# The opening of a transformer block: row statistics and products first on VectorE, PSUM copies by the free engine, values of three groups of heads computed there

## The chip, the cores and the metric

One core of a Trainium2 chip runs the whole kernel. Its engines work from queues of their own and wait for each other by semaphores: TensorE (PE in the profile, its weight loads PEld) multiplies matrices into PSUM, VectorE (DVE), ScalarE (ACT) and GpSimd (POOL) compute, and SyncE (SP) issues the transfers. The metric is the device time of one execution in microseconds (us): 1263.09 us before, the median of three runs (1261.11 to 1264.53).

## The reference

A pre-norm transformer block over 2048 tokens of width 1024, 32 heads of 32 columns, feed-forward width 3584, all tensors bf16:

```python
x = A_x
h = x + attention(layernorm(x), wqkv, wo)     # softmax(q k^T / sqrt(32)) v, all 32 heads
h2 = h + gelu(layernorm(h) @ w1 + b1) @ w2 + b2
```

The layer norm subtracts the row's mean and divides by the root of its variance plus 1e-5; it has no weights.

## The kernel before, in words

**Tiles and groups.** The tokens are 16 row tiles of 128 (`NT`) and four chunks `tc` of 512 (`NCH`). The 1024 columns of queries, keys and values are eight groups of 128 columns, four heads each (`G`); a group is two pairs of heads. A projection of one group for one chunk is eight matmuls of 512 columns into one PSUM bank and one copy out of it: `proj_k`, `proj_q`, `proj_v`. This text calls it a set. A key set is copied to a staging slot `kst` (five slots, `NKS`), squared on VectorE into `sqk` (L563), and carried by four DMAs to `K2`. A query set is copied to `QT` and squared into `sqq` (L579). A value set is copied to `kst` and turned by one DMA transpose into `V` (L597).

**A planner writes the order.** The Python code does not issue instructions directly. `plan.task` appends each to the list of its engine with the waits that its buffers ask for, and keeps an estimated time at which each engine comes free (`plan.free`). The order on each engine is then fixed, and the engine follows it strictly: an instruction that waits holds up all behind it. Steps that can be placed at leisure lie in chains. `service(t)` goes through the chains in list order and records the first step of each whose inputs and engine are about to be free at the estimated time t.

**The head** is all that happens until the first score matmul. Its parts, in the order of the data:

1. SyncE issues the loads of the 16 row tiles `xr` and of nine weight slots `wk` (L710 to L720).
2. `ln1_batch` (L673) handles two row tiles at a time. Statistics are two halves and an aggregate on VectorE (L455, L457); twelve small steps on GpSimd work out the inverse deviation (L475 to L491), and VectorE takes its reciprocal (L492). Then ScalarE subtracts the mean (L685, 1024 columns) and VectorE multiplies (L688). The chain of the statistics is an ordinary one; the chain of subtract and multiply is put in front of it (`first`).
3. `ln1_tp` (L697) transposes the tile by eight TensorE instructions (L498) into a bank, and ScalarE copies it to `xnT` (L702).
4. When a chunk's four tiles are there, TensorE can do the key set of group 0, in chunk 0 also the query sets of groups 0 to 3, and the value set of group 0. ScalarE copies all of these out of PSUM (L555, L576, L594). The squares L563 and L579 are recorded on VectorE at the moment the set is recorded, behind nothing but what was recorded earlier.
5. `qnorm_a`, `qnorm_b`, `knorm_a` and `knorm_b` make the bound that softmax subtracts: a small matmul over the squares (L608), a maximum on VectorE (L611), a diagonal on VectorE (L619), a matmul that spreads it (L621), and a maximum (L623).

The loop at L741 chooses what TensorE does next: among the candidates in `cands` whose inputs are ready, the lowest number goes first (0 the transposes, 1 keys and norms, 2 queries, 3 values). It ends when the norms of the first queries and of key group 0 are recorded.

**After the head** come four phases, one for each chunk of queries. In a phase, 16 pairs of heads pass, each in 11 units. A unit is three score matmul tiles (L919), one exponential on ScalarE over 1536 columns (L927), and the products with values and with ones (L956). Between them TensorE does filler work out of `fill0` (L780): the rest of the projections, in the order of the groups, one PSUM bank (number 7) being left for it, copied out by VectorE. A pair of group g can't begin before the key norm of group g is there: `qk_prereq` calls `until(("kn", g))`, which does filler work without a pause until it is. In phases 1 to 3 the filler is the output projection and feed-forward of the chunk before; the last feed-forward is the tail.

Of the kernel before, what the change touches and what calls it, by code (L numbers as in the profile page):

```python
# [8 lines left out]
ACT = mybir.ActivationFunctionType  # L9
# [4 lines left out]
P = 128  # L14
# [187 lines left out]
def build_kernel(nc, A_x, A_wqkv, A_wo, B_w1, B_b1, B_w2, B_b2, out):  # L202
# [199 lines left out]
    def record_step(ch):  # L402
        eng, fn, reads, writes, cost = ch.steps.popleft()
        if eng == "mark":
            if fn not in marks:
                until(fn)
        elif eng == "call":
            fn()
        else:
            plan.task(eng, fn, reads=reads, writes=writes, cost=cost)  # L410
# [7 lines left out]
    def service(t):  # L418
        again = True
        while again:  # L420
            again = False
            for ch in list(chains):
                eng, fn, reads, writes, cost = ch.steps[0]
                if eng == "mark":
                    ok = fn in marks
                elif eng == "call":
                    ok = plan.ready(E.SP, reads, writes) <= t
                else:
                    r = plan.ready(eng, reads, writes)
                    if eng == E.DVE:  # L430
                        ok = plan.free[eng] <= t + 250 and r <= t + 250
                    else:
                        ok = r <= max(plan.free[eng], t)
                if ok:
                    record_step(ch)
                    again = True
                    if not ch.steps:
                        chains.remove(ch)

    def chain(steps, first=False):  # L440
        ch = Chain(steps)
        if first:
            k = sum(1 for c_ in chains if c_.first)
            chains.insert(k, ch)
            ch.first = True
        else:
            chains.append(ch)
        return ch
# [60 lines left out]
    def group(mms, evac, reads_of, n=512, chunk=2, chs=()):  # L509
        bank = fbanks.next()  # L510
        k = len(mms)
        for i, (lhsT, rhs) in enumerate(mms):
# [7 lines left out]
            if i == k - 1:  # L520
                evac(bank)


    wslot = {}
    wfree = deque(range(NWK))
    worder = deque([("k", 0)] + [("q", g) for g in range(4)] + [("v", 0)]
                   + [(k_, g) for g in range(1, 4) for k_ in "kv"] + [("q", g) for g in range(4, 8)]
                   + [(k_, g) for g in range(4, 8) for k_ in "kv"] + [("Q", g) for g in range(G)])

    def load_next():  # L530
# [14 lines left out]

    kscount = [0]

    def proj_k(g, tc, eng="dve"):
        s = wslot[("k", g)]

        def evac(bank):
            ks = kscount[0] % NKS
            kscount[0] += 1
            if eng == "act":
                act(lambda a: a.activation(kst[:, ks, :], ps[:, bank, :], ACT.Copy), reads=[B_ps[bank]], writes=[B_kst[ks]], cost=600)  # L555
            else:
                dve(lambda v: v.tensor_copy(kst[:, ks, :], ps[:, bank, :]), reads=[B_ps[bank]], writes=[B_kst[ks]], cost=690)
            src = kst[:, ks, :].rearrange("p (a b c) -> p a b c", a=2, b=2)
            for pr in range(2):
                for par in range(2):  # L560
                    dma(K2[64 * par:64 * par + 64, 2 * g + pr, 2 * tc:2 * tc + 2, :], src[64 * pr:64 * pr + 64, :, par, :], 32768,
                        reads=[B_kst[ks]], writes=[B_K2h[2 * g + pr][tc][par]], lanes=lanes_q)
            dve(lambda v: v.tensor_tensor(sqk[:, tc, :], kst[:, ks, :], kst[:, ks, :], ALU.mult),  # L563
                reads=[B_kst[ks]], writes=[B_sqk[tc]], cost=420)
            marks.add(("k", g, tc))

        yield from group([(wk[:, s, dc, :], xnT[tc][:, dc, :]) for dc in range(DC)], evac,
                         lambda i: [B_wk[s]] + xn_of(tc))

    def proj_q(g, tc, eng="dve", late=None, key="q"):  # L570
        s = wslot[(key, g)]
        w_, B_w, q2, B_q2 = (wk, B_wk, sqq, B_sqq) if late is None else late

        def evac(bank):
            if eng == "act":
                act(lambda a: a.activation(QT[:, QS[tc], g, :], ps[:, bank, :], ACT.Copy), reads=[B_ps[bank]], writes=[B_QT[tc][g]], cost=600)  # L576
            else:
                dve(lambda v: v.tensor_copy(QT[:, QS[tc], g, :], ps[:, bank, :]), reads=[B_ps[bank]], writes=[B_QT[tc][g]], cost=690)
            dve(lambda v: v.tensor_tensor(q2[:, g % 4, :], QT[:, QS[tc], g, :], QT[:, QS[tc], g, :], ALU.mult),  # L579
                reads=[B_QT[tc][g]], writes=[B_q2[g % 4]], cost=420)  # L580
            marks.add(("q", g, tc))

        yield from group([(w_[:, s, dc, :], xnT[tc][:, dc, :]) for dc in range(DC)], evac,
                         lambda i: [B_w[s]] + xn_of(tc))

    def proj_v(g, tc, eng="dve"):

        s = wslot[("v", g)]

        def evac(bank):  # L590
            ks = kscount[0] % NKS
            kscount[0] += 1
            if eng == "act":
                act(lambda a: a.activation(kst[:, ks, :], ps[:, bank, :], ACT.Copy), reads=[B_ps[bank]], writes=[B_kst[ks]], cost=600)  # L594
            else:
                dve(lambda v: v.tensor_copy(kst[:, ks, :], ps[:, bank, :]), reads=[B_ps[bank]], writes=[B_kst[ks]], cost=690)
            dma_t(V[:, tc * 4:tc * 4 + 4, g * P:(g + 1) * P], kst[:, ks, :], 131072, [B_kst[ks]], [B_V[tc * 4 + t][g] for t in range(4)])  # L597
# [75 lines left out]
    def ln1_batch(tiles):  # L673
# [3 lines left out]
            st += ln_stats_steps(s_, tt % 4, xrt[tt], B_xr[tt])  # L677
        lo, hi = tiles[0] % 4, tiles[-1] % 4 + 1
        k = s_ * 2 + lo // 2
        rs = ln_rstd_steps(s_, lo, hi, E.Pool, -1.0)  # L680

        def spawn():
            for tt in tiles:
                x_ap, B_x, i = xrt[tt], B_xr[tt], tt % 4
                chain([(E.Activation, lambda a, x_ap=x_ap, i=i: a.activation(x_ap, x_ap, ACT.Identity, bias=lnf[:, s_, i, 0:1], scale=-1.0),  # L685
                        [B_x, B_lnm[k]], [B_x], 1080),
                       ("mark", ("rs", k), [], [], 0),
                       (E.DVE, lambda v, x_ap=x_ap, i=i: v.tensor_scalar(x_ap, x_ap, rstd[:, s_, i:i + 1], None, ALU.mult),  # L688
                        [B_x, B_rstd[k]], [B_x], 430),
                       ("call", lambda tt=tt: normed.add(tt), [], [], 0) if tt < TP else  # L690
                       ("call", lambda tt=tt: ln1_t(tt), [B_x], [B_xnTf[tt]], 0)], True)
        chain(st + rs[:1] + [("call", spawn, [], [], 0)] + rs[1:] + [("call", lambda: marks.add(("rs", k)), [], [], 0)])

    TP = 16
    normed = set()

    def ln1_tp(tt):  # L697
# [1 line left out]
        bank = fbanks.next()  # L699
        yield Need([B_xr[tt]], [B_ps[bank]])  # L700
        tp = transposes(lambda k: xrt[tt][:, k * P:(k + 1) * P], [B_xr[tt]], bank, DC)
        act(lambda a: a.activation(xnT[tc][:, :, t4 * P:(t4 + 1) * P], tp.rearrange("p (dc t) -> p dc t", dc=DC), ACT.Copy),  # L702
            reads=[B_ps[bank]], writes=[B_xnTf[tt]], cost=980)
        marks.add(("xn", tt))

    def ln1_t(tt):
        dma_t(xnT[tt // 4][:, :, (tt % 4) * P:(tt % 4 + 1) * P], xrt[tt], 262144, [B_xr[tt]], [B_xnTf[tt]])
        marks.add(("xn", tt))

    for tt in range(4):  # L710
# [7 lines left out]
        load_x(tt)  # L718
    for _ in range(4):
        load_next()  # L720
    for tt in range(0, NT, 2):
        ln1_batch([tt, tt + 1])

    cands = []
    for tt in range(TP):
        cands.append((0, lambda tt=tt: tt in normed, [B_xr[tt]], ln1_tp(tt)))
    for tc in range(NCH):
        def got(tc=tc):
            return all(("xn", t_) in marks for t_ in range(tc * 4, tc * 4 + 4))
        cands.append((1, got, xn_of(tc), proj_k(0, tc, "act")))  # L730
        if tc == 0:
            for g in range(4):
                cands.append((2, got, xn_of(tc), proj_q(g, 0, "act")))
    cands.append((1, lambda: all(("q", g, 0) in marks for g in range(4)), B_sqq, qnorm_a(0, 0)))
    cands.append((1, lambda: B_qn[0].w is not None, [B_qn[0]], qnorm_b(0, 0)))
    cands.append((1, lambda: all(("k", 0, tc) in marks for tc in range(NCH)), B_sqk, knorm_a(0)))
    cands.append((1, lambda: B_kn[0].w is not None, [B_kn[0]], knorm_b(0)))
    for tc in range(NCH):
        cands.append((3, lambda tc=tc: all(("xn", t_) in marks for t_ in range(tc * 4, tc * 4 + 4)), xn_of(tc), proj_v(0, tc, "act")))
    clock = 0.0  # L740
    while ("kn", 0) not in marks or ("qn", 0, 0) not in marks:  # L741
        clock = max(clock, plan.free[E.PE])
# [12 lines left out]
        if ("q", 0, 0) in marks:  # L755
            qd_load(0, 0)
            qd_load(0, 1)
    v_left = [c_[3] for c_ in cands if c_[0] == 3]
    with_b = [("b1", b1bf, B_b1, Bf_b1bf), ("b2", b2bf, B_b2, Bf_b2bf)]
    for _, t_, src, B_ in with_b:  # L760
        dma(t_[:], src.rearrange("(c p) -> p c", p=P), 8192, writes=[B_], lanes=lanes_a, noncontig=True)
# [18 lines left out]
    def fill0():  # L780
        for key in [("k", 0)] + [("q", g) for g in range(4)]:
            used(key)
        for gen in v_left:
            yield from gen
        used(("v", 0))

        def keys(g, side=()):
            side = deque(side)
# [4 lines left out]
            used(("k", g))  # L793

        def values(g):
            for tc in range(NCH):
                yield from proj_v(g, tc)
                if tc < 2:
                    yield from (knorm_a, knorm_b)[tc](g)
            used(("v", g))  # L800

        for g in range(1, 4):
            yield from keys(g)
# [708 lines left out]
```

## Time and profile before

| | us |
|---|---|
| median of three runs | 1263.09 |
| the profiled execution | 1257.86 |
| its span, first to last instruction | 1255.6 |
| first transposes on TensorE | 10.91 |
| first projection matmul | 17.23 |
| first score matmul (end of the head) | 61.28 |
| first exponential | 62.02 |
| first exponential of phase 1 | 326.45 |
| TensorE busy over the span | 1171.9 |
| ScalarE busy over the span | 1120.8 |
| VectorE busy over the span | 636.6 |

Times in the profile are from the span's start. A timeline row gives the start, the duration, the engine, the line, what is written and read, and in brackets how long the engine was idle before it and what released it. Rows of like instructions in sequence are merged (x2 and so on). A table by windows gives each engine's busy time in stretches of the span, with the number of instructions in parentheses; PEclk is the granted TensorE clock as a share of full speed, and the last columns are the busy share of the DMA engines and GB/s. Durations overlap where an engine pipelines, so the distance from start to start is the cost of an instruction in a row of them.

### The profile page before, as it was taken

The numbers are of one execution on the slowest core, as the hardware profiler recorded it, in microseconds if no ns is written. First come the engines' busy times: TensorE is split into PE (matmuls) and PEld (weight loads), VectorE is DVE, ScalarE is ACT, GpSimd is POOL, SyncE is SP. The second block draws the span as 40 slices with busy tenths as digits, with TensorE's granted clock in tenths as the row PEclk, the third lists the DMA queues.
The fourth block names the chain that finished last, engine by engine and source line by source line (L and its number), as shares of the span: only waits on it lengthen the run. The fifth ranks groups of instructions, "written<-read, shape, count | busy, mean of one in ns | idle before, by whom it ended". The sixth has DMA issues, their size and how long they took to land.

```text
span 1255.6 us, 22538 instructions
## 1 busy us (share of the span) xinstructions
PE 1171.9 (93%) x9066; PEld 399.6 (32%) x9232; DVE 636.6 (51%) x1181; ACT 1120.8 (89%) x914; POOL 36.0 (3%) x180
## 2 busy tenths in 40 slices
PE   5699998999999999999999999999999999997998
PEld 3333322333233333333333332333222323333444
DVE  6524444444465878222366884222568842236820
ACT  6799997999999999999999999999999999962831
POOL 3300000000010000000010000000100000000000
PEclk9899999999999999999999999999999999997999
DMA  7162222223341324343623251342223513334733
GB/s 222 28 129 64 60 61 62 58 59 80 101 68 55 93 72 118 76 114 77 177 47 93 77 151 39 76 121 71 63 76 90 138 35 80 97 85 134 193 89 92
DMA packets 316056, 113.70 MB, mean 91 GB/s; under 512 B 235568, under 2 KB 313392, under 8 KB 315952
## 3 DMA queue, kind: packets, MB, share of 16 engines
q1 hardware_dynamic: 315952, 112.25, 35.8%
q8 instruction: 73, 1.20, 0.4%
q14 instruction: 31, 0.25, 0.1%
HBM read 84.94 MB, written 4.19 MB: 71 GB/s over the span
## 4 chain that ended last, share of the span: by engine, by line
PE 77%; DVE 8%; ACT 8%; issue 6%; DMA 1%; POOL 0%; DVEq 0%; SPq 0%; ACTq 0%
PE ps L518 29%; PE ps L956 16%; PE ps L1251 15%; PE ps L919 15%; ACT PT L927 6%; DVE xh L1218 1%; DVE lnst L455 1%; ACT tm L1227 1%; DVE Rg L976 1%; DVE QT L986 0%; DVE tm L1225 0%; PE ps L498 0%; DVE Sg L969 0%; DVE rcp L979 0%; DVE tm L1224 0%
## 5 line engine op out<-in xcount | busy, mean ns | idle before, releaser
L927 ACT ACTIVATE PT<-ps,biasm 128x1536 bf16<-128x1536 f32 (+1 forms) x704 | 996.6, 1545 | 24.5 <-PE ps L919 21.6
L956 PE MATMUL ps<-PT,ones 128*32 128x512 bf16 x2048 | 285.7, 384 | 0.0
L956 PE MATMUL ps<-PT,V 128*32 128x512 bf16 x2048 | 285.4, 384 | 0.3
L919 PE MATMUL ps<-Qd,K 32*128 32x512 bf16 x2048 | 274.6, 386 | 8.4 <-ACT PT L927 6.3
L518 PE MATMUL ps<-hnT,w 128*128 128x512 bf16 x629 | 165.8, 382 | 9.3 <-issue 3.5
L1251 PE MATMUL ps<-gT,w 128*128 128x512 bf16 x629 | 166.2, 381 | 6.2 <-issue 5.2
L919 PEld LDWEIGHTS ps<-Qd,K 32*128 32x128 bf16 x2048 | 68.0, 91 | 292.7 <-issue 149.1
L956 PEld LDWEIGHTS ps<-PT,V 128*32 128x32 bf16 x2048 | 77.0, 95 | 142.0 <-issue 95.2
L969 DVE COPY Sg<-ps 128x512 f32<-128x512 f32 x64 | 44.3, 692 | 152.9 <-PE ps L956 152.9
L518 PE MATMUL ps<-xnTe,wk 128*128 128x512 bf16 x357 | 94.2, 387 | 6.4 <-issue 1.7
L1218 DVE TENSOR_SCALAR xh<-ps,b1f 128x512 bf16<-128x512 f32 x84 | 62.9, 749 | 50.4 <-PE ps L518 49.5
L518 PEld LDWEIGHTS ps<-hnT,w 128*128 128x128 bf16 x672 | 52.5, 97 | 90.4 <-issue 38.4
L1251 PEld LDWEIGHTS ps<-gT,w 128*128 128x128 bf16 x672 | 51.7, 97 | 81.9 <-issue 36.5
L956 PEld LDWEIGHTS ps<-PT,ones 128*32 128x32 bf16 x2048 | 77.3, 95 | 0.2
L1258 DVE TENSOR_SCALAR oT<-ps,b2f 128x512 bf16<-128x512 f32 x24 | 18.0, 749 | 105.8 <-PE ps L1251 105.7
L518 PE MATMUL ps<-xnTl,wk 128*128 128x512 bf16 x240 | 63.6, 390 | 4.8 <-ACT xnTl L702 1.8
L1228 DVE SCALAR_TENSOR_TENSOR gT<-tm,xh 128x512 bf16<-128x512 bf16 x84 | 57.3, 685 | 5.8 <-ACT tm L1227 5.4
L1225 DVE SCALAR_TENSOR_TENSOR tm<-tm,xh 128x512 bf16<-128x512 bf16 x84 | 58.0, 690 | 2.3
L1227 ACT ACTIVATE tm<-tm 128x512 bf16<-128x512 bf16 x84 | 55.4, 659 | 2.9 <-DVE tm L1225 2.4
L518 PE MATMUL ps<-hnT,w_t 128*128 128x512 bf16 x219 | 50.9, 393 | 1.6 <-ACT hnT L1186 1.2
L1251 PE MATMUL ps<-gT,w_t 128*128 128x512 bf16 x219 | 48.4, 379 | 0.3
L518 PEld LDWEIGHTS ps<-xnTe,wk 128*128 128x128 bf16 x384 | 31.6, 99 | 52.8 <-issue 21.5
(104 smaller groups left out, 790.8 us busy)
## 6 DMA issues: line engine op xcount, KB each, us to landing
w<-in_B_w_dram SPq DMA_DIRECT2D x42, 512.0 KB, 3.8
w<-in_B_w_dram SPq DMA_DIRECT2D x24, 896.0 KB, 5.5
wk<-in_A_wqkv_dram SPq DMA_DIRECT2D x32, 256.0 KB, 3.1
Qd<-QT SPq DMA_DIRECT2D x128, 64.0 KB, 2.6
w_t<-in_B_w_dram SPq DMA_DIRECT2D x14, 512.0 KB, 3.8
w_t<-in_B_w_dram SPq DMA_DIRECT2D x8, 896.0 KB, 5.0
xr<-in_A_x_dram SPq DMA_DIRECT2D x16, 256.0 KB, 4.9
K<-kst SPq DMA_DIRECT2D x128, 32.0 KB, 1.9
```

The lines of the kernel that those rows point to most:

```text
L455: steps.append((E.DVE, lambda v, c=c: v.bn_stats(lnst[:, s, i, c * 6:(c + 1) * 6], x_ap[:, c * 512:(c + 1) * 512]), [B_x], [B], 690))
L518: pe(lambda p, i=i, lhsT=lhsT, rhs=rhs: p.matmul(ps[:, bank, 0:n], lhsT, rhs, start=(i == 0), stop=(i == k - 1)), reads=reads_of(i), write ...
L919: pe(lambda p, kt=kt, rg=rg, b=b, o=o: p.matmul(ps[:, s0 + b, o:o + w], K2[32 * rg:32 * rg + 32, p_, kt // 2, :], Qd[32 * rg:32 * rg + 32, ...
L927: act(lambda a: a.activation(PT[:, o_, 0:nb, 0:wa], ps[:, s0:s0 + nb, 0:wa], ACT.Exp, bias=biasm[:, g, tc:tc + 1], scale=SCALE), reads=wr ...
L956: pe(lambda p, c0=c0, lhsT=lhsT, uu=uu, b=b, o=o: p.matmul(ps[c0:c0 + 32, OD, 0:w], lhsT, PT[:, uu % NPT, b, o:o + w], start=start, stop=stop,
L969: dve(lambda v: v.tensor_copy(Sg[:, pr, 0:w], ps[:, OD, 0:w]), reads=[B_ps[OD]], writes=[B_Sg[pr]], cost=690)
L1218: dve(lambda v: v.tensor_scalar(xh[:, gs, 0:w], ps[:, bank, 0:w], b1f[:, fc:fc + 1], 0.5, ALU.add, ALU.mult), reads=[B_ps[bank], Bf_b1f], ...
L1225: st.append((E.DVE, lambda v: v.scalar_tensor_tensor(tm[:, gs, 0:w], tm[:, gs, 0:w], GB, xh[:, gs, 0:w], ALU.add, ALU.mult), [Bt, Bx], [Bt ...
L1227: st.append((E.Activation, lambda a: a.activation(tm[:, gs, 0:w], tm[:, gs, 0:w], ACT.Tanh, scale=GK), [Bt], [Bt], 180 + .75 * w))
L1228: st.append((E.DVE, lambda v: v.scalar_tensor_tensor(gT[:, fc, 0:w], tm[:, gs, 0:w], 1.0, xh[:, gs, 0:w], ALU.add, ALU.mult), [Bt, Bx], [B ...
L1251: pe(lambda p, fc=fc, s=s, bank=bank: p.matmul(ps[:, bank, 0:w], w2[:, s, fc, :], gT[:, fc, 0:w], start=(fc == 0), stop=(fc == FC - 1)), r ...
L1258: dve(lambda v, bank=bank, db=db: v.tensor_scalar(oT[:, db, 0:w], ps[:, bank, 0:w], b2f[:, db:db + 1], None, ALU.add), reads=[B_ps[bank], ...
```

## The change

- Statistics chains go into the list's front part, batch by batch, and the subtract-and-multiply chains of a batch stand just behind its own statistics (`behind=mine`). The squares become ordinary chains (`square(..., later=True)`), so every statistics, subtract or multiply step stands before them.
- The batches are of 2, 2, 4, 4, 2 and 2 tiles instead of eight of 2. The first and the last compute the inverse deviation on VectorE, all eleven steps at once; the others on GpSimd.
- While statistics are left, ScalarE subtracts and copies as before. When they are all recorded (`stats_left[0] == 0`), a subtraction, a copy of transposes and a copy of a set go to whichever of VectorE and ScalarE comes free first by the planner.
- The value sets of groups 0, 1 and 2 (`HV = 3`, twelve sets) are candidates in the head, with numbers 3, 4 and 5, instead of the four sets of group 0; their weights are loaded before those of key group 1. What the head does not reach stays in `v_left` for `fill0`.

```diff
-    def chain(steps, first=False):
+    def chain(steps, first=False, behind=None):
         ch = Chain(steps)
         if first:
-            k = sum(1 for c_ in chains if c_.first)
+            k = sum(1 for c_ in chains if c_.first) if behind is None else chains.index(behind) + 1
             chains.insert(k, ch)
...
+                elif callable(eng):
+                    e_ = eng()
+                    ok = plan.ready(e_, reads, writes) <= max(t + 100, plan.free[e_]) and plan.free[e_] <= t + 300
...
+    HV = 3
-    worder = deque([("k", 0)] + [("q", g) for g in range(4)] + [("v", 0)]
-                   + [(k_, g) for g in range(1, 4) for k_ in "kv"] + [("q", g) for g in range(4, 8)]
+    worder = deque([("k", 0)] + [("q", g) for g in range(4)] + [("v", g) for g in range(HV)]
+                   + [(k_, g) for g in range(1, 4) for k_ in "kv" if k_ == "k" or g >= HV] + [("q", g) for g in range(4, 8)]
...
+    BATCH = [(0, 2), (2, 4), (4, 8), (8, 12), (12, 14), (14, 16)]
+    def out_of(bank, dst, B_dst, src=None, costs=(600, 690)):
+        src = ps[:, bank, :] if src is None else src
+        if not stats_left[0] and plan.free[E.DVE] < plan.free[E.Activation]:
+            dve(lambda v: v.tensor_copy(dst, src), reads=[B_ps[bank]], writes=B_dst, cost=costs[1])
+        else:
+            act(lambda a: a.activation(dst, src, ACT.Copy), reads=[B_ps[bank]], writes=B_dst, cost=costs[0])
+    def square(sq, src, B_src, B_sq, mark, later):
+        step = (E.DVE, lambda v: v.tensor_tensor(sq, src, src, ALU.mult), [B_src], [B_sq], 420)
+        if later:
+            chain([step, ("call", lambda: marks.add(mark), [], [], 0)])
...
-        rs = ln_rstd_steps(s_, lo, hi, E.Pool, -1.0)
+        last = tiles[-1] == NT - 1
+        own = last or tiles[0] == 0
+        rs = ln_rstd_steps(s_, lo, hi, E.DVE if own else E.Pool, -1.0)
+        def counted():
+            stats_left[0] -= len(tiles)
+        def sub(tt):
...
+            if sub_eng() == E.DVE:
+                dve(lambda v: v.tensor_scalar(x_ap, x_ap, lnf[:, s_, i, 0:1], -1.0, ALU.subtract, ALU.mult), ...
+            else:
+                act(lambda a: a.activation(x_ap, x_ap, ACT.Identity, bias=lnf[:, s_, i, 0:1], scale=-1.0), ...
...
+        mine = chain(st + [("call", counted, [], [], 0)] + (at_once(rs) if own else rs[:1]) + [("call", spawn, [], [], 0)] + ([] if own else rs[1:])
+              + [("call", lambda: marks.add(("rs", k)), [], [], 0)], True)
+    def sub_eng():
+        return E.DVE if not stats_left[0] and plan.free[E.DVE] < plan.free[E.Activation] else E.Activation
...
-    for tt in range(0, NT, 2):
-        ln1_batch([tt, tt + 1])
+    for lo, hi in BATCH:
+        ln1_batch(list(range(lo, hi)))
...
-    cands.append((1, lambda: all(("k", 0, tc) in marks for tc in range(NCH)), B_sqk, knorm_a(0)))
+    cands.append((1, lambda: all(("k2", 0, tc) in marks for tc in range(NCH)), B_sqk, knorm_a(0)))
...
-    for tc in range(NCH):
-        cands.append((3, lambda tc=tc: all(...), xn_of(tc), proj_v(0, tc, "act")))
+    for g in range(HV):
+        for tc in range(NCH):
+            v_cands[(g, tc)] = proj_v(g, tc, True)
+            cands.append((3 + g, lambda tc=tc: all(...), xn_of(tc), v_cands[(g, tc)]))
...
-    v_left = [c_[3] for c_ in cands if c_[0] == 3]
+    v_left = [[c_[3] for c_ in cands if c_[0] == 3 + g] for g in range(HV)]
...
         def values(g):
-            for tc in range(NCH):
-                yield from proj_v(g, tc)
-                if tc < 2:
-                    yield from (knorm_a, knorm_b)[tc](g)
-            used(("v", g))
+            vs = v_left[g] if g < HV else [proj_v(g, tc) for tc in range(NCH)]
+            side = deque([knorm_a(g), knorm_b(g)])
+            for gen in vs:
+                yield from gen
+                if side:
+                    yield from side.popleft()
+            while side:
+                yield from side.popleft()
+            if vs:
+                used(("v", g))
```

## The prediction

> **What bounds the kernel now.** I read the slices of the page first, then the head by windows, then the timelines of the engines in it, and last the exponentials after it. The slices:
>
> ```profile
> PE   5699998999999999999999999999999999997998
> ACT  6799997999999999999999999999999999962831
> ```
>
> After the first two slices of 31.4 us each, TensorE and ScalarE are both nearly full until the tail. What starts earlier ends earlier there, and a set that TensorE no longer has to do leaves room. The head is the exception:
>
> ```profile
> 17.23:27.86 10.63, 10.58 (x40) 4.41 (x42) 3.45 (x10) 6.27 (x8) 3.43 (x17) 1.00 0.78 209
> 27.86:38.97 11.11, 8.69 (x77) 5.11 (x76) 9.10 (x24) 8.65 (x11) 2.74 (x14) 1.00 0.10 23
> 38.97:48.31 9.34, 3.78 (x33) 3.47 (x35) 7.13 (x17) 8.53 (x10) 5.87 (x28) 0.65 0.09 21
> 48.31:61.28 12.97, 10.25 (x52) 4.52 (x53) 2.75 (x7) 7.19 (x9) 1.17 (x7) 0.86 0.12 28
> ```
>
> The columns are window, length, and the busy time of TensorE, its weight loads, VectorE, ScalarE and GpSimd. TensorE is busy 33.3 of the 44.05 us from the first projection to the first score matmul, part of it at a granted clock of 0.65 and 0.86. VectorE's timeline shows why:
>
> ```profile
> 17.50 0.64 DVE L455 BATCH_NORM_STATS2 lnst<-xr 128x6 f32<-128x512 bf16 x1
> 21.47 0.42 DVE L563 TENSOR_TENSOR sqk<-kst 128x512 bf16<-128x512 bf16 x1 [3.33 <-ACT kst L555]
> ...
> 30.02 0.69 DVE L455 BATCH_NORM_STATS2 lnst<-xr 128x6 f32<-128x512 bf16 x1
> ...
> 46.45 0.20 DVE L457 BATCH_NORM_AGGREGATE lnmv<-lnst 128x2 f32<-128x12 f32 x1
> 52.17 0.42 DVE L563 TENSOR_TENSOR sqk<-kst 128x512 bf16<-128x512 bf16 x1 [5.51 <-ACT kst L555]
> ```
>
> Tile 8 has its first half of statistics at 17.50 and its second at 30.02. Between them VectorE waits in order at squares whose copies don't exist yet. The last load of x is issued at 14.8 and lands within 6.0, so data isn't what is late. The statistics end at 46.65, the head 14.6 later. Last, ScalarE's exponentials:
>
> ```profile
> 157.37 28.09 ACT L927 ACTIVATE PT<-ps,biasm 128x1536 bf16<-128x1536 f32 x20 [0.19 <-PE ps L919]
> 196.80 31.00 ACT L927 ACTIVATE PT<-ps,biasm 128x1536 bf16<-128x1536 f32 x22 [11.35 <-PE ps L919]
> 229.08 31.00 ACT L927 ACTIVATE PT<-ps,biasm 128x1536 bf16<-128x1536 f32 x22 [1.28 <-PE ps L919]
> ```
>
> Up to unit 88, the start of the ninth pair, they run without a gap; there ScalarE waits 11.35 us for key group 4, whose sets come too late. TensorE then does four sets one after another, each waiting for the copy of the last out of the single bank:
>
> ```profile
> 183.73 1.90 PE L518 MATMUL ps<-xnTl,wk 128*128 128x512 bf16 x8
> 186.41 1.90 PE L518 MATMUL ps<-xnTl,wk 128*128 128x512 bf16 x7 [0.79 <-DVE kst L557]
> 189.19 1.89 PE L518 MATMUL ps<-xnTe,wk 128*128 128x512 bf16 x8 [0.88 <-DVE kst L557]
> ```
>
> From start to start a set costs 2.7 us there (2.68 and 2.78). Later groups wait 1.28 each. So each set done in the head beyond today's four is worth 2.7 us at this place, for four sets at most (10.07 of the 11.35).
>
> **Part 1, statistics first.** VectorE's work until the last statistics, if nothing blocks: it starts at 3.35; a tile costs 1.53 (starts at 4.93 and 6.46), 16 of them 24.5. New on it is the inverse deviation of the first batch: eleven steps in the tail run from 1142.97 to 1145.13, 2.16 us. Ten products at 0.44 (two in 0.88) and four reciprocals at 0.17 fall between: 5.1. The end is 3.35 + 24.5 + 2.16 + 5.1 = 35.1 instead of 46.65.
>
> The front of the head pays for it. Tiles 0 and 1 have their reciprocal at 6.46 + 2.16 = 8.6 instead of 10.2, but VectorE does this before the statistics of tiles 2 and 3, which end at 8.6 + two products 0.9 + 3.06 = 12.6 instead of 9.6. GpSimd's chain of 3.25 (6.61 to 9.86), the products 0.9, a half statistics of 0.7 in between, a tile's transposes at the slow clock 0.95, ScalarE's last copy 1.0 and some eight handovers of 0.1 give about 20.2 for the first chunk, where it was 17.2. Call this S; between 18.5 and 21.
>
> **Part 2, ScalarE, and the choice of the free engine.** ScalarE starts at 6.9 and lacks work for about 4.9 us before S. With 12 subtractions at 1.07, 12 copies of transposes at 0.97 and ten copies of sets at 0.6 (30.4) the fourth chunk is complete at 42.2 at the earliest, if VectorE takes the last four tiles. A VectorE copy of this size takes 0.69 in the tail, no dearer than ScalarE's. From the last copy to the first score matmul it took 5.3 us before (56.02 to 61.28). A value set in front of the last key set can't be broken off: up to 1.73 more. ScalarE and VectorE thus allow an end of the head at 47.5 to 49.2. The last batch's deviation on VectorE costs 2.16 instead of GpSimd's 3.25; that gain is in this sum. The deferred squares, 8 at 0.42 = 3.4, lie in the time when ScalarE is the later one; without that cover they cost up to 3.4.
>
> **Part 3, TensorE in the head.** Its own sum comes out later, so it decides. A set costs 1.73 at full clock, from the copies of the queries:
>
> ```profile
> 26.33 0.60 ACT L576 ACTIVATE QT<-ps 128x512 bf16<-128x512 f32 x1 [1.13 <-PE ps L518]
> 28.05 0.60 ACT L576 ACTIVATE QT<-ps 128x512 bf16<-128x512 f32 x1 [1.13 <-PE ps L518]
> ```
>
> Behind S stand eight key and query sets (13.8), twelve tiles of transposes at 0.53 (two in 1.06; 6.4), four norm matmuls (1.25), and the slow start, which the chain of waits shows in these two pieces:
>
> ```profile
> 17.23 5.83 PE ps L518 x17
> 23.11 4.93 PE ps L518 x22
> ```
>
> 17 matmuls at 0.343 and 22 at 0.224: 17 x 0.127 = 2.2 us lost, which comes again, since TensorE again has nothing to do before S. The sum is 23.7. With n value sets and i us of waits the head ends at H = 20.2 + 23.7 + 1.73 n + i. For the kernel before, 17.2 + 23.7 + 4 x 1.73 = 47.8 against 61.28: it lost i = 13.5. After the change TensorE has value sets to do from about 30 us on (six once two chunks are there), so most waits are filled. Left are those it has entered: at the two spreads it stood 1.89 and 1.09 for VectorE, 3.0 together, and VectorE is fuller now. The lower bound of i is 0, the upper the 13.5 of before; I take 3, the row of the same wait. Of n I take 4: the planner counts 216 ns for each matmul and knows no slow start, so it sees some 2 to 4 us more room than the sum above, two sets beyond the one or two that 49.2 would allow. The idle time that is to hold twelve sets is largely the idle time that part 1 removes.
>
> **Other queues.** SyncE gets the four value transposes as before, 1.28 each, and nothing more while n is 4; at n = 12 it has 12 x 1.28 + 16 key DMAs at 0.63 + 2.5 for the queries = 28 us in some 30. Weight loads keep their number, nine; key group 1 is in the ninth slot. In the later phases the planner's filler quota starts from a count of eight sets too many in place of none (24 matmuls, 5.2 us); ScalarE is full there, so I set it at nothing, with 2 us either way.
>
> GpSimd's steps slow where a product runs: they take 0.19 to 0.20, but next to the products at 42.14
>
> ```profile
> 42.19 0.49 POOL L477 TENSOR_SCALAR lny<-lnf 128x2 int32<-128x2 int32 x1
> 42.76 0.38 POOL L480 TENSOR_TENSOR lnt<-lny 128x2 f32<-128x2 f32 x1
> ```
>
> That is 0.25 for each product; with up to four products beside a chain of 3.25 us it is 1.0, within the bounds of S. The Trainium skill (SBUF — State Buffer, Who interferes with whom) speaks against more VectorE work here: GpSimd shares a port pair with VectorE instructions of some kinds, and the second one blocks until the first is through. By that, four products of 0.47 would hold a chain up for 1.9 and S would be 21.1.
>
> **The sum.** Head: 61.28 - H = 17.4 - 1.73 n - i. Ninth pair: 2.7 (n - 4). Together 6.6 + 0.97 n - i, for n up to 8. With n = 4 and i = 3: H = 53.8, the wait of 11.35 stays, the gain is 7.5. The profiled execution of 1257.86 would be 1250.4. The median of the runs is 5.2 above that execution; the gain is taken from the median: 1255.6.
>
> **Rivals.**
> - *The value sets do fit.* ScalarE has them copied and TensorE barely waits: n = 8, i = 0 to 3: H = 57.7 to 60.7, the long wait gone, gain 11.4 to 14.4, or 1248.7 to 1251.7. For it: TensorE's 10.75 idle us from 17.23 on. Against: part 1 moves the end of the head into just these. If S also comes at 18.5 it is 1247.
> - *No difference.* i = 7 to 14: TensorE stands at diagonals and at banks that ScalarE hasn't emptied; ScalarE's 40.4 us in the head get 0.6 more for each additional set. Gain within 3.8 either way (0.3%, about what a measurement tells from no change).
> - *Slower.* ScalarE's queue becomes the bound: VectorE by the planner's times is never the freer engine, so ScalarE does all: 16 x 1.07 + 16 x 0.97 + (8 + n) x 0.6, from 6.9 with 4.9 idle. For n = 4 that is 51.6, and 7.0 behind it 58.6; each further us of standing adds one. It decides from H = 65.1 on, i = 14.3; at i = 16 the time is 1268.6. Against it: this needs 6.5 us of standing beyond ScalarE's whole work.
>
> **Chances and range.** Forecast (gain 3.8 to 11, 1252 to 1259) 0.50; sets fit 0.17; no difference 0.20; slower 0.13. The range from 1246.5 to 1264 takes the first two and most of the third. Faster 0.67, same 0.20, slower 0.13.
>
> **What the profile will show.** The last L455 near 35 instead of 45; a first projection at 20, later than before; first score matmul near 54; four value copies before it (2 to 6); a wait of about 11 before unit 88; everything behind shifted alike. Wrong would be: a first score matmul behind 58, seven or more value copies ahead of it, or a gain that arises after 330 us.

## The result, and the profile after

The median went from 1262.11 us (now of four runs) to 1245.70 us. The ratio is 0.9872, with a 95% interval from 0.9848 to 0.9896: 13 to 19 us of gain where 7.5 had been forecast. The profiled execution took 1248.98 us with a span of 1247.2. The slices of the page after:

```profile
PE   4999999998999999999999999999899999987998
ACT  5699999999999999999999999999999999952831
```

TensorE's digit is 9 in the second slice, where it was 6. The head by the same windows as before:

```profile
17.23:27.86 10.63, 9.31 (x56) 5.07 (x56) 8.46 (x19) 7.31 (x9) 2.40 (x12) 1.00 0.73 198
27.86:38.97 11.11, 11.06 (x70) 5.79 (x70) 9.94 (x32) 10.22 (x14) 5.21 (x24) 1.00 0.20 49
38.97:48.31 9.34, 9.23 (x79) 5.70 (x79) 7.98 (x18) 8.46 (x9) 0.00 (x0) 1.00 0.25 58
48.31:61.28 12.97, 11.88 (x70) 4.81 (x69) 5.31 (x15) 4.48 (x7) 0.00 (x0) 1.00 0.27 61
```

TensorE (first busy column) is busy for 41.5 of the 44.05 us, at a granted clock of 1.00, where it had 33.3 busy us and a clock down to 0.65. (The slow start isn't seen in that column: the first 23 projection matmuls took 6.80 us, where 23 at 0.216 would be 5.0.) VectorE's timeline in the head of the changed kernel, and rows of ScalarE's behind it:

```profile
17.15 0.68 DVE L458 BATCH_NORM_STATS2 lnst<-xr 128x6 f32<-128x512 bf16 x1
...
36.28 0.21 DVE L460 BATCH_NORM_AGGREGATE lnmv<-lnst 128x2 f32<-128x12 f32 x1
...
42.94 0.47 DVE L713 TENSOR_SCALAR xr<-xr,lnf 128x1024 bf16<-128x1024 bf16 x1
```
```profile
45.65 1.14 ACT L716 ACTIVATE xr<-xr,lnf 128x1024 bf16<-128x1024 bf16 x1
47.35 1.02 ACT L563 ACTIVATE xnTl<-ps 128x1024 bf16<-128x1024 bf16 x1 [0.56 <-PE ps L501]
...
56.39 0.60 ACT L563 ACTIVATE kst<-ps 128x512 bf16<-128x512 f32 x1 [4.11 <-PE ps L521]
```

The statistics end at 36.5 instead of 46.65. But only one of the sixteen subtractions falls to VectorE (the row at 42.94); ScalarE's last one starts at 45.65, and the fourth chunk is complete at 50.2. TensorE fills the time until then with value sets: nine stand ahead of the first score matmul, which comes at 58.51 and not much sooner than before. What has gone is the wait behind it. ScalarE's exponentials of phase 0:

```profile
59.24 30.74 ACT L990 ACTIVATE PT<-ps,biasm 128x1536 bf16<-128x1536 f32 x22
...
165.59 19.52 ACT L990 ACTIVATE PT<-ps,biasm 128x1536 bf16<-128x1536 f32 x14 [0.40 <-PE ps L982]
185.42 14.64 ACT L990 ACTIVATE PT<-ps,biasm 128x1536 bf16<-128x1536 f32 x10 [0.30 <-PE ps L982]
```

The ninth pair begins at 185.42 after 0.30 us of idling, where it had been 11.35. Phase 1 begins at 313.06 instead of 326.45.

### The profile page after: what moved, and what is told of

The parts are those of the page before. It is cut to its first block, busy times and chain, and to the rows that moved or that the text cites. A ratio compares the mean times of both kernels' runs of the same rounds, so it can differ in the third digit from the quotient of the medians.

```text
span 1247.2 us, 22514 instructions
## 1 busy us (share of the span) xinstructions
PE 1169.1 (94%) x9070; PEld 400.4 (32%) x9232; DVE 641.8 (51%) x1203; ACT 1118.2 (90%) x910; POOL 26.9 (2%) x132
## 4 chain that ended last, share of the span: by engine, by line
PE 77%; DVE 10%; ACT 6%; issue 5%; SPq 2%; DMA 1%; DVEq 0%; POOL 0%; ACTq 0%
PE ps L521 29%; PE ps L1314 16%; PE ps L1019 16%; PE ps L982 14%; ACT PT L990 5%; SPq L254 2%; DVE Rg L1039 1%; DVE xh L1281 1%; DVE QT L1049 1%; DVE lnst L458 1%; PE ps L501 1%; DVE Rg L1045 1%; DVE rcp L1042 1%; DMA Qd<-QT 0%; DVE kst L582 0%
## 5 line engine op out<-in xcount | busy, mean ns | idle before, releaser
L521 PEld LDWEIGHTS ps<-xnTe,wk 128*128 128x128 bf16 x384 | 31.7, 98 | 51.7 <-issue 21.2
```

The source lines that it names most:

```text
L521: pe(lambda p, i=i, lhsT=lhsT, rhs=rhs: p.matmul(ps[:, bank, 0:n], lhsT, rhs, start=(i == 0), stop=(i == k - 1)), reads=reads_of(i), write ...
```

## The experiments

One table for all. "Sets" are the value sets done ahead of the first score matmul; a half stands for four of a set's eight matmuls. "Phase 1" is its first exponential in the profile, and the two columns before it are TensorE's busy and other time up to there, which add up to it but for rounding. Up to phase 1 the kernels with eleven sets did two sets more of the projections than the others (by the weight loads for `xnTe`, 384 against 368), 3.5 us of their busy time. Ratios are against the kernel before on the same chip.

One row's busy and other time can't be held against the rest. Most traces lack some 44 matmul records up to phase 1 (the changed kernel's has 2290 for 2334 weight loads); that of "the same, two groups" lacks 4 (2337 for 2341), and so shows more busy time for the same work: in phase 1, equally long in both, 261.1 us against the 255.7 of "values of two groups". In the last row 144 matmuls of no use are part of the busy time.

| kernel | sets | first projection | first score matmul | busy | other | phase 1 | median us | ratio (95%) |
|---|---|---|---|---|---|---|---|---|
| before | 4 | 17.2 | 61.3 | 286.5 | 39.9 | 326.4 | 1262.1 | |
| before, again | 4 | 17.4 | 61.3 | 286.2 | 40.3 | 326.5 | 1262.6 | 1.0011 (0.9999 to 1.0024) |
| changed | 9 | 20.1 | 58.5 | 281.3 | 31.7 | 313.1 | 1245.7 | 0.9872 (0.9848 to 0.9896) |
| changed, again | 9 | 20.2 | 60.0 | 282.7 | 31.4 | 314.1 | 1246.3 | 0.9878 (0.9858 to 0.9898) |
| values of one group | 4 | 20.3 | 54.5 | 283.2 | 36.4 | 319.6 | 1253.9 | 0.9934 (0.9916 to 0.9953) |
| old order, values of three | 11 | 17.6 | 68.3 | 289.5 | 31.3 | 320.8 | 1259.2 | 0.9974 (0.9959 to 0.9990) |
| squares at once | 10 | 20.2 | 63.4 | 284.7 | 28.5 | 313.2 | 1246.2 | 0.9875 (0.9854 to 0.9896) |
| first batch on GpSimd | 8.5 | 17.8 | 54.6 | 281.5 | 28.0 | 309.5 | 1241.5 | 0.9854 (0.9835 to 0.9873) |
| first batch on GpSimd, again | 8.5 | 17.9 | 55.3 | 282.2 | 28.0 | 310.2 | 1240.8 | 0.9842 (0.9818 to 0.9866) |
| ScalarE copies all | 11 | 20.0 | 65.7 | 288.5 | 30.3 | 318.8 | 1255.7 | 0.9950 (0.9932 to 0.9967) |
| the same, two groups | 8.5 | 20.1 | 65.8 | 290.7 | 30.6 | 321.3 | 1253.8 | 0.9935 (0.9921 to 0.9948) |
| values of two groups | 7.5 | 20.2 | 57.6 | 283.0 | 31.1 | 314.1 | 1246.6 | 0.9888 (0.9873 to 0.9903) |
| one-step normalization | 7.5 | 17.6 | 53.3 | 282.4 | 27.2 | 309.6 | 1242.1 | 0.9852 (0.9834 to 0.9869) |
| first batch on GpSimd, warm TensorE | 9 | 17.9 | 54.6 | 288.9 | 19.4 | 308.3 | 1243.0 | 0.9849 (0.9827 to 0.9872) |

### The two halves, each alone

Statistics and copies as changed, values of one group only:

```diff
-    HV = 3
+    HV = 1
```

> The changed kernel with HV = 1: statistics first and the free engine stay, but only the four value sets of group 0 are done in the head. Theory A (TensorE is full in the head, and each value set done there beyond four is worth about 2.7 us at the ninth pair): the head ends at 20.05 + 23.7 + 4 x 1.73 = 50.7 us or a little later (up to 55), 4 to 8 us before the 58.5 of the changed kernel, but the wait of about 11 us for key group 4 is back; in all 5 to 9 us slower than the changed kernel, about 1250 to 1255. Theory B (the order of the statistics brings the gain, the value sets are only moved): equal to the changed kernel, about 1246, and no wait of more than 2 us at the ninth pair. Theory C (the value sets bring it all): near the kernel before, about 1260.

Theory A held: the head ended at 54.5, the long wait was back, and the time was 7.6 to 8.2 us above the changed kernel's. The exponentials of this run at the ninth pair and two pairs later:

```profile
189.99 31.00 ACT L990 ACTIVATE PT<-ps,biasm 128x1536 bf16<-128x1536 f32 x22 [11.35 <-PE ps L982]
222.26 31.00 ACT L990 ACTIVATE PT<-ps,biasm 128x1536 bf16<-128x1536 f32 x22 [1.28 <-PE ps L982]
```

These are the waits of before to the hundredth. This kernel is the forecast made true: four sets, the wait unchanged, the gain all from the head (6.8 us at the first exponential and still 6.8 at phase 1; 8 in the timed runs, where 7.5 was said). So the forecast's sum was right for four sets, and the number of sets was not.

The other half alone, on the kernel before:

```diff
+    HV = 3
...
-    for tc in range(NCH):
-        cands.append((3, lambda tc=tc: all(...), xn_of(tc), proj_v(0, tc, "act")))
+    for g in range(HV):
+        for tc in range(NCH):
+            cands.append((3 + g, lambda tc=tc: all(...), xn_of(tc), proj_v(g, tc, "act")))
```

> The kernel before with only the value sets of groups 0 to 2 made candidates in the head (and their weights loaded first); statistics, batches, squares and copies as before. Eleven value sets stand ahead of the first score matmul. Theory A: TensorE's idle 10.75 us and its slow clock in the head of before hold most of the seven further sets (12.1 us), so the head ends at 60 to 65 and the wait at the ninth pair is gone: 6 to 13 us faster than before, 1249 to 1256. Theory B: no gain, 1260 to 1264, because the head gets longer by what the wait gives back. Theory C: equal to the changed kernel, about 1246.

It gained 3 us, less than theory A had it and more than B; C fell. The wait at the ninth pair is gone, but the head ends at 68.3. Its TensorE, at three places:

```profile
37.74 3.34 PE L518 MATMUL ps<-xnTe,wk 128*128 128x512 bf16 x8
...
52.49 7.49 PE L518 MATMUL ps<-xnTl,wk 128*128 128x512 bf16 x28 [0.22 <-issue]
...
68.28 0.39 PE L930 MATMUL ps<-Qd,K 32*128 32x512 bf16 x3
```

Eight matmuls take 3.34 us here and 1.9 at full clock; 28 take 7.49 where they would take 6.1. The old order of the statistics still makes TensorE wait, and after the waits it works slowly: busy time up to phase 1 is 289.5 against 281.3 in the changed kernel, of which 3.5 is work done ahead. Phase 1 still begins 5.6 us earlier than before, but from there on this profile needs 935.1 us against 929.2 (phase 2 alone 268.0 against 263.9); no run shows why. The two halves bring 8 and 3 us alone and 15.6 to 16.4 together.

### The changed kernel and the kernel before, again

> The changed kernel once more, unaltered, for a narrower interval and a second profile. In the first pair of profiles phase 1 begins 13.3 us earlier than before, but the span ends only 8.4 earlier; the medians of the runs differ by 16.4. If the later phases lose something by the change, the gain at the end is again smaller than that at the start of phase 1 by about 5 us. If the profiled execution was a chance one, the end is 12 to 16 us earlier and the timed gain is 12 to 17 us.

> The kernel before, unaltered, for a second profile of it. The first one (1257.86) lies 4 us below the median of its timed runs, and the gain by profiles (9 to 12 us) is smaller than the gain by timed runs (15 to 16). If the first profile was a quick execution by chance, the second has a span 2 to 5 us longer, and the difference lies where the granted clock is below full speed. If a profiled execution of this kernel is regularly quicker than a timed one, it has the same span within 1 us. Timed, it is equal to itself.

Timed, both repeated (1246.28; 1262.61, ratio to itself 1.0011 from 0.9999 to 1.0024). The second profile of the changed kernel has a span of 1243.8, 3.4 shorter than the first, although its head was 1.5 longer; from phase 1 on it needs 929.6 instead of 934.1. The kernel before needs 929.2 and 928.8 there. The 5 us lost behind phase 1 in the first profile were therefore that execution's own.

The second profile of the kernel before has a span of 1255.3, the first 1255.6, and its profiled executions (1257.86 and 1257.54) lie 3 to 5 us below its medians (1260.75 to 1262.61 in all sets), at the lower end of its timed runs (1257.6 to 1266.0). Those of the changed kernel (1248.98 and 1245.58) lie on either side of its medians (1245.70 and 1246.28). The profiles show 12.3 to 13.4 us of gain at phase 1 and 8.1 to 11.8 at the end of the span, so that some 3 of the 16 us of the timed gain don't show at phase 1. Two things on record bear on them. A run of the kernel before takes 2.2 us longer than its span, one of the changed kernel 1.8. And the quick runs of the kernel before are those with the higher granted clock: of the sixteen beside this one, the quickest took 1257.60 at 0.990 and the slowest 1266.00 at 0.983, while the eight runs of the changed kernel all lie at 0.987 to 0.989. That the clock is the cause was not tested.

### The squares

```diff
-            square(sqk[:, tc, :], kst[:, ks, :], B_kst[ks], B_sqk[tc], ("k2", g, tc), head)
+            square(sqk[:, tc, :], kst[:, ks, :], B_kst[ks], B_sqk[tc], ("k2", g, tc), False)
```

and the same for the queries.

> The changed kernel with the squares recorded at once instead of as late chains; all else stays. If in-order waits at squares are what held up the statistics, VectorE's last statistics end some 5 to 11 us later than the 36.3 of the changed kernel and the first score matmul 2 to 5 us later; ten value sets instead of nine are done in the head, and the time is 2 to 4 us longer (1248 to 1250). If the front place of the statistics in the list is enough by itself, the time is equal to that of the changed kernel within 1.5 us.

The first part came: the last statistics end at 46.3, as late as before the change, the head at 63.4. But the time is 1246.22, equal to the changed kernel's. VectorE waits at a square again, and phase 0 has nearly no gap:

```profile
24.47 0.43 DVE L566 TENSOR_TENSOR sqk<-kst 128x512 bf16<-128x512 bf16 x1 [3.39 <-ACT kst L563]
```
```profile
143.35 141.61 ACT L990 ACTIVATE PT<-ps,biasm 128x1536 bf16<-128x1536 f32 x101 [0.24 <-PE ps L982]
```

The head is 3.4 to 4.9 us later here, but a tenth set is done in it, and phase 1 begins at the same time. From the first exponential to phase 1 ScalarE takes 249.0 us; its own work is 248 (22 units in 31.0). The end of the head alone is no measure: a later one is paid back as long as TensorE works meanwhile and ScalarE has gaps left. The deferral of the squares makes the head shorter and brings nothing in the end. VectorE's waits at squares, back in this kernel, therefore don't bound it.

### The first batch on GpSimd

```diff
-        own = last or tiles[0] == 0
+        own = last
```

> The changed kernel with the inverse deviation of the first batch on GpSimd again (only the last batch has it on VectorE). The statistics of tiles 2 and 3 then aren't held up by 2.16 us, and the first projection comes at 17.3 to 18 us instead of 20.1. Theory A (what counts is the time in which TensorE does no work before phase 1, since from the first projection on it is full): 2 to 3 us less of it, phase 1 begins near 311 instead of 313 to 314, and the time is 1 to 4 us shorter than that of the changed kernel. Rival: TensorE waits for later tiles instead, because ScalarE has no more room; then the time is equal within 1 us.

Theory A held, a little beyond its 1 to 4 us, and this version beats both kernels: 1241.54, in a repetition beside the kernel further below 1240.75 (0.9842 from 0.9818 to 0.9866), 4 to 5 us under the changed kernel's medians. The first projection comes at 17.84, 2.2 to 2.4 us earlier, and phase 1 begins 2.9 to 4.6 earlier; from the first projection to the first score matmul TensorE now idles for 0.37 us instead of 1.30. TensorE of this version at the start of the projections:

```profile
14.45 2.19 PE L501 MATMUL ps<-ident,xr 128*128 128x128 bf16 x16 [1.57 <-DVE xr L721]
17.84 8.79 PE L521 MATMUL ps<-xnTe,wk 128*128 128x512 bf16 x31 [1.20 <-ACT xnTe L563]
```

VectorE's own eleven steps for the first two tiles sped up these two by 1.6 us and held up the statistics of all others by 2.1; the first chunk needs four tiles.

### ScalarE alone, with three groups and with two

```diff
-        if not stats_left[0] and plan.free[E.DVE] < plan.free[E.Activation]:
+        if False:
...
-        return E.DVE if not stats_left[0] and plan.free[E.DVE] < plan.free[E.Activation] else E.Activation
+        return E.Activation
```

> The changed kernel without the choice of the free engine: ScalarE does every subtraction and every copy out of PSUM in the head, as before the change. Eleven value sets stand ahead of the first score matmul. Theory A: the head ends 3 to 6 us later (62 to 65), but TensorE has value sets to do meanwhile, so phase 1 begins within 1.5 us of the changed kernel's and the time is equal within 2 us. Rival (the free engine is what makes the head work): TensorE stands at banks that ScalarE hasn't emptied, its time without work before phase 1 grows by more than 3 us over the 31.5 of the changed kernel, and the time is 3 to 7 us longer.

The rival's time (9 to 10 us more), but not by its mechanism: TensorE's time without work before phase 1 is 30.3, not more than in the changed kernel. Only 4.7 to 5.7 of the 9 to 10 us lie ahead of phase 1: two sets are done earlier (3.5 us), and work is slower, since TensorE waits 0.99 and 1.12 us for the last tile and then takes 5.31 us for 16 matmuls, at a granted clock of 0.67:

```profile
58.23 5.31 PE L521 MATMUL ps<-xnTl,wk 128*128 128x512 bf16 x16 [1.12 <-ACT xnTl L563]
```

Behind phase 1 this profile needs 936.8 us against 929.6 and 934.1; why is open. I then held the number of sets to be the cause, and took the third group away (HV = 2):

> As the kernel in which ScalarE does all subtractions and copies, but with HV = 2, so that 8 value sets are done in the head instead of 11. There the head ended at 65.7 us, and from the first exponential phase 0 took 252.4 us, hardly more than ScalarE's own 248 (176 units at 1.409): ScalarE bounds phase 0 and each later start is lost. Theory D (too many sets in the head: beyond some seven they only push the first exponential back): the head ends at 59 to 62, phase 1 begins at 313 to 316, and the time is 5 to 9 us shorter than the 1255.7 of eleven sets, 1247 to 1250. Rival (ScalarE's doing all the copies costs the time by itself): within 2 us of 1255.7, with phase 1 at 318 or later.

That theory fell. With eight and a half sets the head ends at 65.8 as with eleven, and 2 us are gained instead of 5 to 9. TensorE of this second kernel:

```profile
54.67 0.86 PE L501 MATMUL ps<-ident,xr 128*128 128x128 bf16 x8 [2.71 <-DVE xr L721]
56.65 6.12 PE L521 MATMUL ps<-xnTl,wk 128*128 128x512 bf16 x16 [1.11 <-ACT xnTl L563]
```

The last tile comes late from ScalarE (its last subtraction starts at 52.95, its last copy of transposes at 55.57, against 45.65 and, on VectorE, 49.52). TensorE waits 2.71 and 1.11, and does the next 16 matmuls in 6.12 us; in the changed kernel 16 of them took 3.62. The wait of 3.8 us costs another 2.5 by the slow clock after it (granted 0.58 from 56.65 to 62.70). So the free engine is worth 6 to 7 us with two groups and 9 to 10 with three. Without it the fourth chunk is complete at 56.6 and 58.2, with it at 50.0 and 50.2.

Read as steps from the kernel before, the twelve candidates alone bring 3 us, with the order of the statistics, the batches and the deviations on VectorE 6, and with the free engine 16. The sizes of the batches and the last batch's deviation on VectorE were not run alone.

### Values of two groups

> The changed kernel with HV = 2: eight value sets may be done in the head, seven and a half are. Theory A: TensorE has enough to do with two groups' sets; the head ends 2 to 3 us earlier, the wait at the ninth pair stays below 2 us, and the time is equal to the changed kernel's within 1.5 us. Rival: the ninth set is worth its 2.7 us as the ones before it: 2 to 4 us longer than the changed kernel.

Theory A held. Seven and a half sets are done in the head, and the ninth pair's wait is 1.38 us:

```profile
184.43 31.01 ACT L990 ACTIVATE PT<-ps,biasm 128x1536 bf16<-128x1536 f32 x22 [1.38 <-PE ps L982]
216.71 31.01 ACT L990 ACTIVATE PT<-ps,biasm 128x1536 bf16<-128x1536 f32 x22 [1.27 <-PE ps L982]
```

From four sets to seven (with the half, seven and a half) the wait fell by 9.97, 3.3 (2.8) us for each; the head became 3.1 us longer. What is done beyond that brings nothing that a measurement shows.

### One-step normalization

```diff
...
-                chain([(sub_eng, lambda tt=tt: sub(tt), [B_xr[tt], B_lnm[k]], [B_xr[tt]], 0),
-                       ("mark", ("rs", k), [], [], 0),
+                chain([("mark", ("rs", k), [], [], 0),
...
-            dve(lambda v: v.tensor_scalar(x_ap, x_ap, rstd[:, s_, i:i + 1], None, ALU.mult), reads=[B_x, B_rstd[k]], writes=[B_x], cost=430)
+            dve(lambda v: v.tensor_scalar(x_ap, x_ap, lnf[:, s_, i, 0:1], rstd[:, s_, i:i + 1], ALU.subtract, ALU.mult),
+                reads=[B_x, B_lnm[k], B_rstd[k]], writes=[B_x], cost=500)
```

> As the kernel with the first batch on GpSimd, and in addition the normalization in one VectorE step (subtract the mean and multiply by the inverse deviation together, as the tail does it in 0.50 us a tile), so that ScalarE's sixteen subtractions (17 us) fall away. The intermediate rounding of the difference to bf16 falls away with them. Theory A: TensorE was already full from the first projection on, so 17 us less on ScalarE bring nothing beyond the earlier first projection: 1 to 4 us faster than the changed kernel, 0 to 2 faster than the kernel with the first batch on GpSimd. Rival (ScalarE bounds the head): 4 to 8 us faster than the changed kernel.

Theory A held: 1242.05, equal to the version with the first batch on GpSimd. Sixteen subtractions less on ScalarE end the head 1.4 us earlier with one value set less done in it, and phase 1 begins at the same time.

### A warm TensorE

The version with the first batch on GpSimd, with matmuls of no use ahead of the first projection:

```diff
+    def warm_up(n, after=()):
+        bank = fbanks.next()
+        yield Need([B_ones, B_ident], [B_ps[bank]])
+        for i in range(n):
+            pe(lambda p: p.matmul(ps[:, bank, 0:P], ones_pp[:], ident[:], start=True, stop=True),
+               reads=[B_ones, B_ident] + (list(after) if i == 0 else []), writes=[B_ps[bank]] if i in (0, n - 1) else [], inc=(i == n - 1), cost=60)
+    cands.append((0.5, lambda: B_ident.w is not None, [B_ident, B_ones], warm_up(32)))
+    for tt in range(7):
+        cands.append((0.5, lambda tt=tt: B_lnmv[tt].w is not None, [B_lnmv[tt]], warm_up(16, [B_lnmv[tt]])))
```

> The version with the first batch on GpSimd once more, beside the next kernel on the same chip: 1240 to 1243.

> The version with the first batch on GpSimd, and TensorE does matmuls of no use (ones by identity, 128 columns) while it waits for the first tiles: 32 at the start and 16 after the statistics of each of the tiles 0 to 6. They add nothing to the result. If the slow clock at the start costs 2.2 us of TensorE's work, as the step of the prediction has it, the first 31 projection matmuls take 6.9 us instead of 8.8, the transposes of the first tiles 0.5 instead of 0.95, the first projection comes up to 1 us earlier, and phase 1 begins 2 to 3 us earlier: 1 to 4 us faster than its neighbour. If the added matmuls delay the transposes, or ScalarE bounds phase 0, the gain is 0 to 1 us.

The first projections of this kernel (line 798 is the added matmuls), to be held against the row at 17.84 above:

```profile
14.77 1.07 PE L501 MATMUL ps<-ident,xr 128*128 128x128 bf16 x16 [1.31 <-DVE xr L721]
15.67 2.21 PE L798 MATMUL ps<-ident,ones_pp 128*128 128x128 bf16 x32
17.93 6.85 PE L521 MATMUL ps<-xnTe,wk 128*128 128x512 bf16 x31
```

The slow start is gone: 31 matmuls in 6.85 instead of 8.79, the transposes in half the time. The first projection doesn't come earlier: ScalarE's copy ends at 17.36, 0.34 before its neighbour's, but TensorE has 32 of the added matmuls in front, from 15.67 to 17.88. Phase 1 begins at 308.3, 1.2 to 1.9 us earlier than in the two profiles of its neighbour, and the span is 1237.5 against 1238.9 and 1240.5. The timed runs don't show it: 1242.96 (0.9849 from 0.9827 to 0.9872) against 1240.75, where 1 to 4 us less had been expected. So the term of 2.2 us is near its size on TensorE (1.9), and whether a time can be gained by it stays open.

## Why the prediction was wrong

- **What bounds the head.** VectorE's in-order waits went as forecast, and the last statistics ended at 36.5, where 35.1 was worked out. But that these waits bounded the kernel was only argued: with the squares back in their old place the last statistics end at 46.3 and the time is the same, once the value sets and the free engine are there.
- **The price at the front, S = 20.2** was right: the first projection started at 20.05. The run with the first batch on GpSimd shows the 2.2 to 2.4 us that it costs. GpSimd's steps next to VectorE's products and squares took 0.29 to 0.40 instead of 0.19, four of them in the head of the changed kernel, 0.5 us together. The Trainium skill (SBUF — State Buffer, Who interferes with whom) states a full block of the second instruction; the delay of 1.9 us that I estimated from it was not put to the test, since GpSimd's chain for the tiles 2 and 3 ran from 12.63 to 15.90 with no product beside it.
- **ScalarE's sum, 42.2 for the fourth chunk, is the step that failed.** It was 50.2. I took the chunk to be complete when ScalarE has done its own work and VectorE the last four tiles. The planner's comparison gave VectorE one subtraction: ScalarE did 15 instead of 12 (3.2 us). It also stood 4.0 us after S for TensorE's matmuls and transposes, and the last tile's transposes stood 0.9 behind a set, which the sum had at nothing. From this 42.2 came the end of the head at 47.5 to 49.2, and from that the few sets. From the last copy to the first score matmul it then took 8.3 us, where 5.3 to 7.0 had been set.
- Two runs show that the number of subtractions alone doesn't explain it. Behind the first projection the fourth chunk was complete after 30.2 us in the changed kernel and after 22.0 in the sum. In the one-step kernel ScalarE does no subtraction at all, and it takes 28.1 (VectorE's statistics end at 39.1 there, later than 36.5); seven and a half sets still stood in that head. With values of one group, five sets fewer in TensorE's queue, it takes 27.7. So one engine's own work was the wrong bound for the end of the head; which of the waits between the engines make up the rest stays open.
- **n = 4, i = 3** followed from it and was wrong: n was 9, and i by the same formula is 58.5 - (20.05 + 23.7 + 15.6) = -0.8, or 0.5 in the second profile. Two of the three signs named for being wrong came, a first score matmul behind 58 and seven or more value sets ahead of it. TensorE's sum 23.7 + 1.73 n held; with four sets in place i was 3.6.
- **The wait at the ninth pair "stays"** was therefore wrong. Its price for a set, 2.7, was near: 2.8 to 3.3 measured.
- **The rival "the value sets do fit"** is what happened: head at 57.7 to 60.7 (58.5 and 60.0), the wait gone, gain 11.4 to 14.4 (12.3 to 13.4 at phase 1 by the profiles). Its 1248.7 to 1251.7 is still above the 1245.7 measured, and the range ended 0.8 above it: the further 3 us are as many as those that don't show at phase 1 in the profiles. I gave it 0.17. Against it I had set that an earlier head takes away the idle time that is to hold the sets. That argument needed the head to end early by ScalarE's sum, which was the least certain term.
- **The later phases**, set at nothing with 2 us either way: 934.1 and 929.6 from phase 1 on, against 929.2 and 928.8. In the one execution it was 5.

## What to carry to other kernels

Where one engine is to be full up to some stage, count its work and its time without work up to that stage, and not the moment at which an earlier stage ends: kernels whose heads ended at 57.6 and 63.4 began phase 1 within a microsecond of each other. Work that has no deadline yet is a buffer for the full engine, and the number of pieces that fit follows from how late the feeding chain really is, so bound that lateness from both sides before saying that they don't fit. Bringing the chunks earlier (order and free engine) and filling belong together here: alone they gave 8 and 3 us, together 16.

## What the runs showed of the hardware

A long wait on TensorE can cost twice. After idle stretches of 2.71 and 1.11 us, of 0.99 and 1.12, and of 1.66 and 0.22, the next 16, 16 and 28 matmuls ran at 0.38, 0.33 and 0.27 us each instead of 0.22, at a mean granted clock of 0.58, 0.67 and 0.82; behind the single wait of 1.04 in the changed kernel's head the clock stayed at 1.00. In the three kernels whose heads have such waits and whose traces can be compared (before, old order, ScalarE alone with three groups), TensorE's busy time up to phase 1, without the work done ahead, was some 2 to 3.5 us more than in the kernels with values of one and of two groups (283.2 and 283.0). The Trainium skill (TensorE: Matmul & The Clock Gate, What's actually happening) states half the clock after an idle window of about 3.4 us and full clock after as long a busy one, with windows that run freely. The runs agree in kind, though two waits of 2.1 us together, with transposes of 0.62 between them, were enough here. And the same program did its first 23 projection matmuls in 6.80 us in one execution and in 8.18 in another, a spread of 1.4 us in a part that no edit touched.
